# Linear attention and RWKV channel mix: per-engine orders from a list schedule, five units per four batches, and batch 0's time shift mix folded into the attention weights

## The chip, the cores and the metric

The kernel runs on one core of one Trainium2 chip. The metric is device time in microseconds (us) of the whole program; lower is better. Engines are named as in the profile: PE is TensorE (matmuls), PEld its weight loads, DVE is VectorE, ACT is ScalarE, POOL is GpSimd and SP is SyncE, which here only issues transfers. All times inside a run are counted from the start of its profiled span.

## The reference, cut to what matters

```python
# attention, B=8, H=8, S=576, D=64
q_s = softmax(q, axis=-1)                 # over the 64 features
k_s = softmax(k, axis=2)                  # over the sequence
kv  = einsum('bhsd,bhse->bhde', k_s, v)   # k_s^T v, one 64x64 matrix per head
x   = q_s @ kv                            # then heads side by side: (B, S, 512)
# RWKV channel mix, d_model 512, d_ff 1024
x_prev = x shifted down by one row of the sequence, first row 0
xk = mu_k * x + (1 - mu_k) * x_prev
xr = mu_r * x + (1 - mu_r) * x_prev
k  = maximum(xk @ w_k, 0)
v  = (k * k) @ w_v
out = sigmoid(xr @ w_r) * v
```

Inputs and output are float32. In both kernels the large matmuls take bf16. A batch's heads are handled in two groups (group 0 and 1) of four heads.

## The kernel before: the parts that matter

The order of the work is set by hand. A few lines start batch 0; from then on an attention generator advances by small steps between the matmuls of the channel mix, so that TensorE always has channel-mix work while the other engines prepare the next batch.

```python
    UNITS = ((0, 512), (512, 384), (896, 256))      # columns of two batches (2*576)
...
    # the weights are held back until a load of batch 0, group 0 has landed
    def emit_weights(gate):
        ...
                ld = part(wk_bf, moe_w_k, F, u, 512 * h, 512 * h + 512)
                if gate is not None:
                    tc.add_manual_dep(ld.ins, gate.ins.name, SYNC)
...
    # mu comes from one fp32 transpose of an 8x128 tile
    mup = psum.tile([128, 8], F32, tag="mm", bufs=4, name="mup")
    nc.tensor.transpose(out=mup[:], in_=mu_sb[:], identity=identf[:])
...
    # channel mix: every accumulator is a PSUM tile of its own, four in rotation
    def unit(pair, c0, n, step=1):
        for f0 in range(0, FT, step):
            kfps = [psum.tile([128, 512], F32, tag="mm", bufs=4, name="kfp")
                    for _ in range(step)]
            ...                                             # kfp += wk^T xk
                nc.scalar.activation(out=rel[:, 0:n], in_=kfp[:, 0:n], func=ACT.Relu, ...)
                nc.vector.tensor_tensor(out=k2[:, f0 + i, 0:n], in0=rel..., in1=rel..., op=ALU.mult)
        for m in range(n // 128):
            rp = psum.tile([128, C], F32, tag="mm", bufs=4, name="rp")   # xr wr -> tanh
            ...
            vp = psum.tile([128, C], F32, tag="mm", bufs=4, name="vp")   # k2 wv -> times gate -> out
```

The time shift mix of each head group (`diff`, `mix`) is done on VectorE in bf16: difference of neighbouring rows, scale by mu, add.

The softmax here doesn't subtract the row's maximum and nothing guards it: scores larger than these inputs give would overflow.

Of the kernel before, what the change touches and what calls it, by code (L numbers as in the profile page):

```python
# [15 lines left out]


@with_exitstack
def kernel(
# [12 lines left out]






# [9 lines left out]
    UNITS = ((0, 512), (512, 384), (896, 256))  # L47
    assert B % 2 == 0

    const = ctx.enter_context(tc.tile_pool(name="const", bufs=1))  # L50
    ldpool = ctx.enter_context(tc.tile_pool(name="ldpool", bufs=4))
    apool = ctx.enter_context(tc.tile_pool(name="apool", bufs=3))
    xpool = ctx.enter_context(tc.tile_pool(name="xpool", bufs=2))
    mpool = ctx.enter_context(tc.tile_pool(name="mpool", bufs=2))
    opool = ctx.enter_context(tc.tile_pool(name="opool", bufs=3))
    psum = ctx.enter_context(tc.tile_pool(name="psum", bufs=1, space=bass.MemoryType.PSUM))


    raw = {}

    SYNC = mybir.DependencyInfo(mybir.DependencyClass.Sync, mybir.DependencyReason.DATA)
    ctx.enter_context(tc.manual_schedule(engines={mybir.EngineType.Pool}))

    def emit_load(b: int, g: int, queues=None):
        t = ldpool.tile([128, 3, 2, J * D], F32, tag="raw", name="raw")
        ld = []
        for i, src in enumerate((q, k, v)):
            ap = bass.AP(tensor=src.tensor,
                         offset=src.offset + (b * H + 2 * g) * S * D,
                         ap=[[J * D, 128], [4 * S * D, 2], [1, J * D]])  # L70
            queue = queues[i] if queues else nc.gpsimd
            ld.append(queue.dma_start(out=t[:, i, :, :], in_=ap))  # L72
        raw[b, g] = t
        return ld

    first = emit_load(0, 0, (nc.sync, nc.scalar, nc.sync))
    mu_sb = const.tile([8, 128], F32, name="mu_sb")
    for m, src in enumerate((moe_mu_k, moe_mu_r)):
        ap = bass.AP(tensor=src.tensor, offset=src.offset, ap=[[64, 4], [256, 2], [1, 64]])
        nc.sync.dma_start(out=mu_sb[4 * m:4 * m + 4, :].rearrange("p (u e) -> p u e", u=2),  # L80
                          in_=ap)
    emit_load(0, 1, (nc.scalar, nc.sync, nc.scalar))
    warm = const.tile([1, 1], F32, name="warm")
    nc.vector.memset(warm[:], 0.0)
    nc.scalar.activation(out=warm[:], in_=warm[:], func=ACT.Exp)


    ident = const.tile([128, 128], BF16, name="ident")
    make_identity(nc, ident[:])
    identf = const.tile([8, 8], F32, name="identf")  # L90
    nc.vector.tensor_copy(out=identf[:], in_=ident[0:8, 0:8])
    mask = const.tile([128, 128], BF16, name="mask")
    nc.vector.memset(mask[:], 0.0)
    nc.vector.memset(mask[0:64, 0:64], 1.0)
    nc.vector.memset(mask[64:128, 64:128], 1.0)
    vvs, xbs = [], []
    for i in range(3):
        vv = const.tile([128, J, 130], BF16, name=f"vv{i}")
        nc.vector.memset(vv[:, :, 128:130], 1.0)
        vvs.append(vv)  # L100
        xb = const.tile([128, 2, 64 + S], BF16, name=f"xb{i}")
        nc.vector.memset(xb[:, :, 0:1], 0.0)
        xbs.append(xb)

    wk_bf = const.tile([128, CT, F], BF16, name="wk_bf")
    wv_bf = const.tile([128, FT, C], BF16, name="wv_bf")
    wr_bf = const.tile([128, CT, C], BF16, name="wr_bf")

    def emit_weights(gate):
        def part(dst, src, n, u, c0, c1):  # L110
            ap = bass.AP(tensor=src.tensor, offset=src.offset + 4 * u * D * n + c0,
                         ap=[[n, 64], [D * n, CT], [1, c1 - c0]])
            return nc.gpsimd.dma_start(out=dst[64 * u:64 * u + 64, :, c0:c1], in_=ap)

        for h in range(2):
            for u in range(2):
                ld = part(wk_bf, moe_w_k, F, u, 512 * h, 512 * h + 512)
                if gate is not None:
                    tc.add_manual_dep(ld.ins, gate.ins.name, SYNC)
                gate = None  # L120
        for u in range(2):
            part(wr_bf, moe_w_r, C, u, 0, C)
        n = FT // 2
        for h in range(2):
            ap = bass.AP(tensor=moe_w_v.tensor,
                         offset=moe_w_v.offset + h * n * 128 * C,
                         ap=[[C, 128], [128 * C, n], [1, C]])
            nc.gpsimd.dma_start(out=wv_bf[:, h * n:(h + 1) * n, :], in_=ap)

    mu = const.tile([128, 8], F32, name="mu")  # L130

    def emit_mu():
        mup = psum.tile([128, 8], F32, tag="mm", bufs=4, name="mup")
        nc.tensor.transpose(out=mup[:], in_=mu_sb[:], identity=identf[:])  # L134
        nc.vector.tensor_copy(out=mu[:], in_=mup[:])


    xpair = {}
    box = [0]

    class Attention:
        def __init__(self, b: int, g: int):
            self.b, self.g = b, g
            self.t = raw.pop((b, g))
            self.vv = vvs[box[0] % 3]
            self.xb = xbs[box[0] % 3]
            box[0] += 1
            if b // 2 not in xpair:
                xpair[b // 2] = (xpool.tile([128, CT, 2 * S], BF16, tag="xk", name="xk"),
                                 xpool.tile([128, CT, 2 * S], BF16, tag="xr", name="xr"))  # L150
            self.eqk = apool.tile([128, 2, J, 2, D], BF16, tag="eqk", name="eqk")

        def exp(self, i: int):
            nc.scalar.activation(  # L154
                out=self.eqk[:, i, :, :, :],
                in_=self.t[:, i, :, :].rearrange("p u (j d) -> p j u d", d=D),
                func=ACT.Exp)

        def cast_v(self, copy):
            copy(out=self.vv[:, :, 0:128].rearrange("p j (u d) -> p j u d", u=2),  # L160
                 in_=self.t[:, 2, :, :].rearrange("p u (j d) -> p j u d", d=D))

        def norm_q(self):
            eq = self.eqk[:, 0, :, :, :].rearrange("p j u d -> p (j u) d")
            rsum = apool.tile([128, 2 * J], F32, tag="rsum", name="rsum")
            nc.vector.reduce_sum(out=rsum[:], in_=eq, axis=AX.X)  # L166
            rrec = apool.tile([128, 2 * J], F32, tag="rrec", name="rrec")
            nc.vector.reciprocal(out=rrec[:], in_=rsum[:])
            self.qs = apool.tile([128, J, 128], BF16, tag="qs", name="qs")
            nc.vector.tensor_tensor(  # L170
                out=self.qs[:].rearrange("p j (u d) -> p (j u) d", u=2), in0=eq,
                in1=rrec[:, :, None].to_broadcast((128, 2 * J, D)), op=ALU.mult)

        def kv(self, tag: str):
            if tag == "att":
                t = psum.tile([128, 2, 512], F32, tag="att", bufs=2, name="kvp")
                self.kvp = [t[:, 0, :], t[:, 1, :]]
            else:
                self.kvp = [psum.tile([128, 512], F32, tag="mm", bufs=4, name="kvp")[:, :]
                            for _ in range(2)]  # L180
            for j in range(J):
                for hf in range(2):
                    r = slice(64 * hf, 64 * hf + 64)
                    nc.tensor.matmul(  # L184
                        self.kvp[hf][:, 0:129],
                        lhsT=self.eqk[r, 1, j, :, :].rearrange("p u d -> p (u d)"),
                        rhs=self.vv[r, j, 0:129], start=(j == 0), stop=(j == J - 1))

        def weights(self):
            self.w = apool.tile([128, 2, 128], BF16, tag="w", name="w")  # L190
            rz = apool.tile([128, 2], F32, tag="rz", name="rz")
            for hf in range(2):
                nc.vector.reciprocal(out=rz[:, hf:hf + 1], in_=self.kvp[hf][:, 128:129])
            for hf in range(2):
                nc.vector.scalar_tensor_tensor(  # L195
                    out=self.w[:, hf, :], in0=self.kvp[hf][:, 0:128],
                    scalar=rz[:, hf:hf + 1], in1=mask[:], op0=ALU.mult, op1=ALU.mult)

        def transpose_q(self):
            self.qtp = psum.tile([128, 16, 128], BF16, tag="att", bufs=2, name="qtp")  # L200
            for j in range(J):
                nc.tensor.transpose(out=self.qtp[:, j, :], in_=self.qs[:, j, :],  # L202
                                    identity=ident[:])
# [32 lines left out]
    def attention(b: int, g: int):  # L236
# [11 lines left out]
        yield  # L248
        a.x(0)
        yield  # L250
        a.x(1)
        yield
        a.diff()
        a.mix(0)
# [145 lines left out]
```

## Time and profile before

| | before |
|---|---|
| median of 4 runs beside the changed kernel | 221.03 us (220.99 to 221.58) |
| profiled span | 219.7 us |
| first matmul; first kfp; kfp without a break | 9.79; 20.80; 27.82 us |
| unit 1 of the channel mix starts | 49.66 us |
| last matmul ends | 215.1 us |

The page's second section gives the busy tenths of each engine in 40 slices of 5.5 us. These are four of its rows for the kernel before:

```profile
PE   0156599988999999999999999999999999999991
DVE  1196389999999998889798998888787758483431
ACT  2645279999977779676929696949736392644340
DMA  6999999999999791897085220232131400340414
```

TensorE is full from about 30 us to the end, and not before. So the kernel is bound by TensorE, plus a slow start. The timeline of TensorE shows the start (start, duration, engine, line, what, and in brackets the idle time before it and what ended it):

```profile
9.79 0.24 PE L134 MATMUL mup<-identf,mu_sb 8*128 8x8 f32 x1 [9.79 <-DMA mu_sb<-in_moe_mu_r_dram]
10.56 1.16 PE L184 MATMUL kvp<-vv_103,eqk 64*128 64x129 bf16 x18 [0.53 <-ACT vv_103 L160]
...
20.80 2.77 PE L270 MATMUL kfp<-xk,wk_bf 128*128 128x512 bf16 x6
...
27.82 6.73 PE L270 MATMUL kfp<-xk,wk_bf 128*128 128x512 bf16 x23 [2.92 <-DVE xk L232]
...
49.66 1.14 PE L270 MATMUL kfp<-xk,wk_bf 128*128 128x384 bf16 x6
```

The last step before continuous work is VectorE's mix of batch 0, group 1 (`xk`, 2.92 us of waiting). In what follows, the "lost" time of TensorE means this, worked out from the trace's matmul records: from one matmul's start to the next one's start, less the time that its columns take when warm (columns / 2400 us + 0.0025 us; for the 18 kv matmuls and the 9 transposes of a group 0.035 and 0.068 us each, as they follow each other in the busy part of the trace). Before, TensorE loses 7.8 us in the first 20 us, 7.0 from 20 to 40, 2.7 from 40 to 60 and 4.3 in all the rest.

### The profile page before, as it was taken

The numbers are of one execution on the slowest core, as the hardware profiler recorded it, in microseconds if no ns is written. First come the engines' busy times: TensorE is split into PE (matmuls) and PEld (weight loads), VectorE is DVE, ScalarE is ACT, GpSimd is POOL, SyncE is SP. The second block draws the span as 40 slices with busy tenths as digits, with TensorE's granted clock in tenths as the row PEclk, the third lists the DMA queues.
The fourth block names the chain that finished last, engine by engine and source line by source line (L and its number), as shares of the span: only waits on it lengthen the run. The fifth ranks groups of instructions, "written<-read, shape, count | busy, mean of one in ns | idle before, by whom it ended". The sixth has DMA issues, their size and how long they took to land.

```text
span 219.7 us, 3641 instructions
## 1 busy us (share of the span) xinstructions
PE 193.5 (88%) x1313; PEld 101.6 (46%) x1313; DVE 166.3 (76%) x384; ACT 147.7 (67%) x230; POOL 35.8 (16%) x56
## 2 busy tenths in 40 slices
PE   0156599988999999999999999999999999999991
PEld 0134134534547454445557443546465444554650
DVE  1196389999999998889798998888787758483431
ACT  2645279999977779676929696949736392644340
POOL 1294252433431210230030000000000000000000
PEclk9999969999999999999999999999999999999999
DMA  6999999999999791897085220232131400340414
GB/s 215 397 158 199 262 402 388 393 400 403 404 393 406 273 343 71 256 298 288 3 264 201 49 51 0 57 90 48 36 88 24 95 3 22 73 95 5 108 36 95
DMA packets 16171, 40.62 MB, mean 185 GB/s; under 512 B 2072, under 2 KB 4632, under 8 KB 16152
## 3 DMA queue, kind: packets, MB, share of 16 engines
q0 software_dynamic: 8736, 27.40, 38.0%
q1 hardware_dynamic: 6600, 11.22, 18.0%
q10 hardware_dynamic: 816, 1.77, 2.2%
q8 instruction: 10, 0.16, 0.3%
q14 instruction: 9, 0.07, 0.1%
HBM read 33.56 MB, written 9.44 MB: 196 GB/s over the span
## 4 chain that ended last, share of the span: by engine, by line
PE 60%; ACT 19%; DVE 13%; DMA 3%; issue 2%; SPq 1%; DVEq 0%; ACTq 0%
PE vp L291 22%; PE kfp L270 19%; PE rp L284 11%; ACT eqk L154 5%; ACT qt L207 4%; ACT rel L276 4%; DMA mu_sb<-in_moe_mu_r_dram 3%; PE kvp L184 3%; PE qtp L202 3%; PE xp L212 2%; DVE rsum L166 2%; DVE xk L232 2%; DVE qs L170 2%; ACT xb_105 L215 2%; ACT xb_109 L215 1%
## 5 line engine op out<-in xcount | busy, mean ns | idle before, releaser
L270 PE MATMUL kfp<-xk,wk_bf 128*128 128x384 bf16 (+2 forms) x384 | 72.6, 335 | 4.3 <-DVE xk L232 3.7
L276 ACT ACTIVATE rel<-kfp 128x512 bf16<-128x512 f32 (+2 forms) x96 | 45.4, 518 | 20.5 <-PE kfp L270 19.5
L270 PEld LDWEIGHTS <-wk_bf 128*128 128x128 bf16 x384 | 36.3, 99 | 30.3 <-issue 8.5
L154 ACT ACTIVATE eqk<-raw 128x1152 bf16<-128x1152 f32 x32 | 37.5, 1204 | 9.7 <-DMA raw<-in_q_dram 5.9
L294 DVE SCALAR_TENSOR_TENSOR ot<-th,vp 128x512 f32<-128x512 f32 x36 | 24.6, 683 | 17.3 <-PE vp L291 12.5
L287 ACT ACTIVATE th<-rp 128x512 f32<-128x512 f32 x36 | 22.7, 631 | 21.7 <-PE rp L284 20.7
L284 PE MATMUL rp<-wr_bf,xr 128*128 128x512 bf16 x144 | 37.0, 379 | 0.0
L207 ACT COPY qt<-qtp 128x1152 bf16<-128x1152 bf16 x16 | 18.2, 1136 | 7.7 <-PE qtp L202 7.5
L166 DVE TENSOR_REDUCE rsum<-eqk 128x18 f32<-128x1152 bf16 x16 | 21.6, 1348 | 1.6 <-ACT eqk L154 1.5
L170 DVE TENSOR_TENSOR qs<-eqk,rrec 128x1152 bf16<-128x1152 bf16 x16 | 21.7, 1355 | 0.8
L230 DVE TENSOR_SCALAR xm<-xd,mu 128x576 bf16<-128x576 bf16 x64 | 21.6, 378 | 0.4
L284 PEld LDWEIGHTS <-xr 128*128 128x128 bf16 x144 | 13.3, 98 | 13.8
L72 POOL DMA_DIRECT2D raw<-in_q_dram x14 | 10.0, 713 | 52.9 <-ACT vv_111 L160 24.0
L212 PE MATMUL xp<-qt,w 128*128 128x512 bf16 x64 | 13.5, 302 | 2.6 <-ACT qt L207 2.3
L184 PEld LDWEIGHTS <-eqk 64*128 64x128 bf16 x288 | 9.4, 100 | 9.2 <-issue 8.3
L202 PE MATMUL qtp<-ident,qs 128*128 128x128 bf16 x144 | 11.6, 231 | 1.5 <-DVE qs L170 1.5
L202 PEld LDWEIGHTS <-qs 128*128 128x128 bf16 x144 | 9.8, 103 | 4.1 <-DVE qs L170 1.8
L212 PEld LDWEIGHTS <-w 128*128 128x128 bf16 x64 | 6.3, 103 | 11.0 <-issue 6.1
L72 POOL DMA_DIRECT2D raw<-in_v_dram x14 | 10.0, 711 | 8.4 <-DMA raw<-in_q_dram 5.8
L72 POOL DMA_DIRECT2D raw<-in_k_dram x14 | 10.0, 711 | 5.7 <-DMA raw<-in_v_dram 3.0
L195 DVE SCALAR_TENSOR_TENSOR w<-kvp,rz,mask 128x128 bf16<-128x128 f32 x32 | 9.7, 345 | 0.0
L134 PE MATMUL mup<-identf,mu_sb 8*128 8x8 f32 x1 | 0.2, 243 | 9.8 <-DMA mu_sb<-in_moe_mu_r_dram 9.8
(83 smaller groups left out, 238.7 us busy)
## 6 DMA issues: line engine op xcount, KB each, us to landing
out_dram<-ot SPq DMA_DIRECT2D x72, 128.0 KB, 2.4
raw<-in_q_dram POOLq DMA_DIRECT2D x14, 576.0 KB, 12.4
raw<-in_k_dram POOLq DMA_DIRECT2D x14, 576.0 KB, 12.7
raw<-in_v_dram POOLq DMA_DIRECT2D x14, 576.0 KB, 13.1
wk_bf<-in_moe_w_k_dram POOLq DMA_DIRECT2D x4, 256.0 KB, 6.5
wv_bf<-in_moe_w_v_dram POOLq DMA_DIRECT2D x2, 512.0 KB, 12.4
raw<-in_k_dram ACTq DMA_DIRECT2D x1, 576.0 KB, 5.6
raw<-in_q_dram SPq DMA_DIRECT2D x1, 576.0 KB, 5.2
```

Of the source, the lines that this page charges most:

```text
L72: ld.append(queue.dma_start(out=t[:, i, :, :], in_=ap))
L154: nc.scalar.activation(out=self.eqk[:, i, :, :, :], in_=self.t[:, i, :, :].rearrange("p u (j d) -> p j u d", d=D), func=ACT.Exp)
L166: nc.vector.reduce_sum(out=rsum[:], in_=eq, axis=AX.X)
L170: nc.vector.tensor_tensor(out=self.qs[:].rearrange("p j (u d) -> p (j u) d", u=2), in0=eq, in1=rrec[:, :, None].to_broadcast((128, 2 * J, ...
L202: nc.tensor.transpose(out=self.qtp[:, j, :], in_=self.qs[:, j, :], identity=ident[:])
L207: nc.scalar.copy(out=self.qt[:], in_=self.qtp[:, 0:J, :])
L212: nc.tensor.matmul(self.xp[:, 64 * c:64 * e], lhsT=self.w[:, hf, :], rhs=self.qt[:, c:e, 64 * hf:64 * hf + 64], start=True, stop=True)
L270: nc.tensor.matmul(kfp[:, 0:n], lhsT=wk_bf[:, ct, fc * 128:(fc + 1) * 128], rhs=xk[:, ct, c0:c0 + n], start=(ct == 0), stop=(ct == CT - 1))
L276: nc.scalar.activation(out=rel[:, 0:n], in_=kfp[:, 0:n], func=ACT.Relu, scale=HALF_ROOT)
L284: nc.tensor.matmul(rp[:], lhsT=xr[:, ct, c0 + 128 * m:c0 + 128 * m + 128], rhs=wr_bf[:, ct, :], start=(ct == 0), stop=(ct == CT - 1))
L291: nc.tensor.matmul(vp[:], lhsT=k2[:, ft, 128 * m:128 * m + 128], rhs=wv_bf[:, ft, :], start=(ft == 0), stop=(ft == FT - 1))
L294: nc.vector.scalar_tensor_tensor(out=ot[:], in0=th[:], scalar=1.0, in1=vp[:], op0=ALU.add, op1=ALU.mult)
```

## The change

The intent is to shorten the start and to let a program, not a hand, weave the work.

1. Orders. Every operation goes into a `Plan` with an engine, an assumed occupancy and latency, a priority key, its dependences and the buffers that it takes and gives. A greedy list schedule picks, for each engine, the operation that can start earliest, and among equals the smallest key. The kernel then emits the operations in that order.
2. Units of 512 columns: four of 512 and one of 256 per four batches, in place of 512, 384, 256 per two.
3. Batch 0's mix is folded: the kv weights are multiplied by mu and by (1 - mu), and x and x_prev are summed in PSUM by matmuls. That needs mu spread along the free axis on all 128 partitions, which two sets of small float32 selection matmuls produce.
4. Batch 0's and 1's loads are issued in halves, and mu's load goes first on another queue.

The four single accumulators become halves of two-bank tiles, and the wait of the weight loads on batch 0's load is now only in the plan. Core of the diff, with cuts:

```diff
-    UNITS = ((0, 512), (512, 384), (896, 256))
+    UNITS = ((0, 512), (512, 512), (1024, 512), (1536, 512), (2048, 256))
...
+    banks = [psum.tile([128, 2, 512], F32, name=f"bank_{x}") for x in "abcd"]
+    ps = {"mm": [banks[2 + i // 2][:, i % 2, :] for i in range(4)],
+          "att": [t[:, :, :] for t in banks[0:2]], "early": [t[:, :, :] for t in banks[2:4]]}
...
+    pick = const.tile([8, 8, 2, 128], F32, name="pick")
+    flip = const.tile([1, 2, 128], F32, name="flip")
+    ones = const.tile([1, 64], F32, name="ones")
+    mu_slot = [Slot("mm") for _ in range(3)] + [Slot("att")]
+    def emit_mu_rows(m):
+        for s in range(2):                       # s = 0: mu, s = 1: mu - 1
+            for ct in range(CT):
+                for u in range(2):
+                    nc.tensor.matmul(to, lhsT=pick[:, 4 * m + ct, u, :],
+                                     rhs=mu_sb[:, 64 * u:64 * u + 64], start=True, stop=(s == 0), ...)
+                    if s == 1:
+                        nc.tensor.matmul(to, lhsT=flip[:, u, :], rhs=ones[:],
+                                         start=False, stop=True, ...)
+    for m in range(2):
+        o = plan.add("PE", 2.0, 2.2, -450 + 500 * m, lambda m=m: emit_mu_rows(m), [mu_t],
+                     [mu_slot[1 + m]] + mu_slot[3:] * (m == 0))
...
-                if gate is not None:
-                    tc.add_manual_dep(ld.ins, gate.ins.name, SYNC)
+        wk_done.append(plan.add("POOL", 1.25, 1.25, h, lambda h=h: [
+            weight_part(wk_bf, moe_w_k, F, u, 512 * h, 512 * h + 512) for u in range(2)],
+            gate, size=1048.0))                  # gate: in the plan only
...
+            rank = (max(t, now + 0.03), op.key)  # greedy: earliest start, then key
...
+    for op in plan.order():
+        op.emit()
```

## The prediction

> **What bounds it now.** TensorE, behind a slow start. The windows view has TensorE busy 19.4 to 20.0 of every 20 us from 60 us on. In the timeline a warm 512-column matmul starts every 0.216 us; from the trace's matmul records I get 183.6 us of warm TensorE work: 155 of channel mix and about 1.8 for each of 16 head groups. From 30 us to the last matmul at 215.1 only about 8 us are lost; after unit 1 starts (49.66) 5.9. The tail after the last matmul is 4.6 us, and the measured time is 1.35 above the span.
>
> The rest is the start. mu_sb lands only at 9.7 us, behind bulk loads on its queue; group 1's mix is done at 27.8, and only then is TensorE continuous. Early matmuls come 0.43 us apart, twice the warm 0.216: the half-rate state of an idle array (the Trainium skill, "TensorE: Matmul & The Clock Gate", part 1); the trace agrees.
>
> **What changes.** Batch 0's x copy, edge copy, difference, scale and mix (about 4.5 us in a row after x) become four small vector operations on PSUM (0.35 us each, as the w operation now) and one copy per half and mix. mu no longer queues behind v. q of both groups is loaded first, in halves, so the 1.35 us sums and products start earlier. TensorE gains about 3 us of x matmuls and two sets of 24 fp32 matmuls of 64 columns. The Trainium skill ("FP8 and Floating Point Precision", TensorE Precision Notes) gives true fp32 four passes: 0.107 us warm, 0.21 cold, 2.5 to 5 us a set, an estimate. No run shows it yet. The first set falls in idle time, before 11 us.
>
> Estimated start: batch 0's loads still need until about 12.4 us (590 KB in 1.5 us, read from landings). Then v cast 0.8, kv 1.1, weights 1.3 behind other vector work, x 0.8, copy 0.7: group 1's xk at 18 to 19 instead of 27.8. The first w_k half lands at about 16.
>
> **How much is critical.** Not all 9 us. Unit 1 needs batch 1, whose last load lands at about 36 us as now: 12.3 MB at 0.39 MB/us, unchanged by the diff. Unit 0 with batch 1's attention keeps TensorE busy only to about 41. After the last v come cast, kv, weights, x, copies, edge, difference, scale and mix, 6.4 us bare by the trace's durations, on VectorE and ScalarE that are full between 30 and 60 now. I expect unit 1 at about 44 instead of 49.66, with 2 to 4 us of TensorE wait before it. From there 159.6 us of work, 3 of stalls (VectorE still near 87% full, and batch 3 is needed 192 columns earlier than now), tail 4.6, overhead 1.35: **212.5 us**.
>
> Range 208 to 217. Faster by over 2%: 0.83; within 2%: 0.15; slower: 0.02.
>
> **What would show it.** Right: the first long run of kfp matmuls at 17 to 20 us; a TensorE wait before unit 1 between 40 and 46, released by batch 1's mix; VectorE and ScalarE busy unchanged within 5 us. Wrong: the fp32 matmuls hold TensorE beyond 11 us and delay q transposes and kv; batch 1's loads land later than 38; TensorE loses over 5 us after 60, because the fixed orders rest on assumed durations and in-order queues wait for an operation that the plan thought ready.
>
> **What would make it wrong.** Faster than 208: batch 1 ready near 41, no stalls later. Slower than 217: the order mismatches real landings, so that one late vector operation frees no PSUM bank, or the clock falls to half again in the wait before unit 1.

## The result, and the profile after

| | before | after |
|---|---|---|
| median | 221.03 us | 251.13 us (250.79 to 251.24, 4 runs) |
| ratio | | 1.1345, 95% interval 1.132 to 1.137 |
| profiled span | 219.7 | 249.3 |
| first kfp; unit 1 | 20.80; 49.66 | 38.72; 71.67 |
| last matmul ends | 215.1 | 244.4 |

A ratio here is the mean time of one kernel's fast runs over the mean of the other's fast runs of the same rounds, so it is not quite the ratio of the medians that stand beside it.

The change made the kernel 13.4% slower. The same rows of the page, with the granted clock of TensorE:

```profile
PE   0899889999478999989989998899999999999992
DVE  4920153588997998898999999998944233252331
ACT  4410255699968988998689885566235144244150
PEclk9999999999959999999999999999999999999999
DMA  6999999059999679976510132120240330431413
```

TensorE is busy almost from the start (8 and 9 tenths from the second slice, that is from 6 us; a slice is 6.2 us here), where before it had 1, 5, 6, 5. But VectorE and ScalarE are nearly idle from 12 to 31 us (2, 0, 1 and 1, 0, 2), and the transfer engines stop for one slice (the 0 at about 44 to 50 us). The 5 in the clock row stands for a stretch at half rate around the start of unit 1 (the clock records in the trace say 68.9 to 75.7 us); it comes back below. The kernel before has such a stretch from 27.7 to 31.1 us, in unit 0, and none at unit 1. So TensorE is busy early with something that nobody downstream can use. Its timeline names it:

```profile
7.29 0.24 PE L294 MATMUL bank_c<-identf,mu_sb 8*128 8x8 f32 x1 [7.29 <-DMA mu_sb<-in_moe_mu_r_dram]
7.39 3.65 PE L305 MATMUL bank_c<-mu_sb,pick 8*128 8x64 f32 x16
...
17.80 1.14 PE L419 MATMUL bank_b<-ident,qs_a 128*128 128x128 bf16 x9
18.87 3.67 PE L305 MATMUL bank_d<-mu_sb,pick 8*128 8x64 f32 x16
...
28.74 0.63 PE L309 MATMUL bank_a<-ones,flip 1*128 1x64 f32 x2
29.30 1.16 PE L405 MATMUL bank_c<-vv_a,ek_a 64*128 64x129 bf16 x18
...
38.72 1.03 PE L593 MATMUL bank_c<-xk,wk_bf 128*128 128x512 bf16 x4
...
44.13 1.02 PE L593 MATMUL bank_c<-xk,wk_bf 128*128 128x512 bf16 x4 [0.31 <-ACT rel_b L578]
```

The two sets of float32 selection matmuls run from 7.39 to 17.8 and from 18.87 to 29.3 us; only the nine transposes of one q group stand between them. Batch 0's kv, which came at 10.56 us before, starts at 29.30. The groups by form give the cost (busy us, then mean ns of one recorded instruction):

```profile
L305 PE MATMUL bank_a<-mu_sb,pick 8*128 8x64 f32 x32 | 10.1, 416 | 0.0
L309 PE MATMUL bank_a<-ones,flip 1*128 1x64 f32 x32 | 10.1, 416 | 0.0
```

There are 16 such matmuls of each kind into bank_a in the program, and 32 records: one float32 matmul of 64 columns is two instructions. They start 0.2135 us apart, so one matmul costs 0.427 us of TensorE, a set of 24 takes 10.3 us, both 20.5. The bf16 matmuls around them are at half rate too, as shown further below; no run has these float32 matmuls at full rate. ScalarE shows the second-order damage:

```profile
29.40 0.60 ACT L316 ACTIVATE mu_mask<-bank_a 128x512 f32<-128x512 f32 x1 [15.31 <-PE bank_a L309]
...
42.99 0.60 ACT L578 ACTIVATE rel_a<-bank_c 128x512 bf16<-128x512 f32 x1 [0.66 <-PE bank_c L593]
43.48 0.59 ACT L578 ACTIVATE rel_b<-bank_c 128x512 bf16<-128x512 f32 x1
...
48.95 0.70 ACT L375 ACTIVATE eq_c<-raw_g 128x576 bf16<-128x576 f32 x1
```

The first (1 - mu) mask was complete in PSUM at 17.8 us, but ScalarE reads it only at 29.40, because the second set writes the other half of the same two-bank tile, and everything behind it in ScalarE's order waits too. (This is read from the trace and the code; no run changed it alone while the sets were float32.) Batch 1's first exp (`eq_c`) then stands behind batch 0's relu and starts at 48.95. GpSimd issues the next load into that buffer only afterwards, at 51.56 us after 15.69 us without an issue, which is the hole in the transfers.

There is a second, quieter difference in the last line of TensorE's excerpt. The kfp matmul at 44.13 writes bank_c's half 0. Its previous reader, `rel_a`, ended at 43.59. The matmul waits for `rel_b`, which reads the other half and ends at 44.07.

Finally, the weights are no longer held back. This is GpSimd's timeline, first of the kernel before and then of the changed one:

```profile
9.64 2.62 POOL L113 DMA_DIRECT2D wk_bf<-in_moe_w_k_dram  x4 [8.33 <-DMA raw<-in_v_dram]
```

```profile
3.25 2.51 POOL L333 DMA_DIRECT2D wk_bf<-in_moe_w_k_dram  x4
```

They are issued 6.4 us earlier and share the transfers with batch 0; v of batch 0, group 1 landed at 17.3 us, before at 12.7.

### The profile page after: what moved, and what is told of

It is laid out like the page before. It is cut to its first block, busy times and chain, and to the rows that moved or that the text cites. A ratio compares the mean times of both kernels' runs of the same rounds, so it can differ in the third digit from the quotient of the medians.

```text
span 249.3 us, 3772 instructions
## 1 busy us (share of the span) xinstructions
PE 220.9 (89%) x1377; PEld 120.0 (48%) x1377; DVE 164.7 (66%) x371; ACT 150.1 (60%) x228; POOL 39.2 (16%) x64
## 4 chain that ended last, share of the span: by engine, by line
PE 63%; DVE 16%; ACT 12%; issue 4%; DMA 2%; POOL 0%; DVEq 0%; ACTq 0%; POOLq 0%
PE bank_c L593 11%; PE bank_c L634 10%; PE bank_d L634 9%; PE bank_d L593 9%; PE bank_d L624 6%; PE bank_c L624 4%; PE bank_a L309 3%; PE bank_a L305 3%; DVE qs_a L397 2%; DMA mu_sb<-in_moe_mu_r_dram 2%; PE bank_b L419 2%; ACT rel_b L578 2%; DVE ot_c L640 2%; PE bank_d L305 1%; PE bank_c L305 1%
## 5 line engine op out<-in xcount | busy, mean ns | idle before, releaser
L593 PE MATMUL bank_c<-xk,wk_bf 128*128 128x512 bf16 (+1 forms) x176 | 39.2, 357 | 0.7 <-ACT rel_b L578 0.3
L593 PE MATMUL bank_d<-xk,wk_bf 128*128 128x512 bf16 (+1 forms) x144 | 34.7, 372 | 3.0 <-DVE ot_a L640 0.7
L624 PE MATMUL bank_d<-wr_bf,xr 128*128 128x512 bf16 x84 | 21.5, 378 | 0.9 <-ACT rel_c L578 0.6
L634 PEld LDWEIGHTS <-k_a 128*128 128x128 bf16 x144 | 13.5, 98 | 16.8 <-issue 1.8
L634 PEld LDWEIGHTS <-k_b 128*128 128x128 bf16 x144 | 13.6, 97 | 16.0 <-issue 1.2
L634 PE MATMUL bank_d<-wv_bf,k_a 128*128 128x512 bf16 x72 | 18.3, 379 | 0.9 <-ACT th_b L629 0.6
L634 PE MATMUL bank_d<-wv_bf,k_b 128*128 128x512 bf16 x72 | 18.5, 379 | 0.7 <-ACT th_a L629 0.6
L634 PE MATMUL bank_c<-wv_bf,k_b 128*128 128x512 bf16 x72 | 18.0, 379 | 0.2
L634 PE MATMUL bank_c<-wv_bf,k_a 128*128 128x512 bf16 x72 | 18.0, 379 | 0.0
L624 PE MATMUL bank_c<-wr_bf,xr 128*128 128x512 bf16 x60 | 15.4, 379 | 0.3 <-ACT rel_c L578 0.3
```

Source lines behind the costliest of these rows:

```text
L593: nc.tensor.matmul(bank(kf)[:, 0:n], lhsT=wk_bf[:, ct, fc * 128:(fc + 1) * 128], rhs=xs[0][:, ct, c0:c0 + n], start=(ct == 0), stop=(ct == ...
L624: nc.tensor.matmul(bank(rps), lhsT=xs[1][:, ct, c:c + 128], rhs=wr_bf[:, ct, :], start=(ct == 0), stop=(ct == CT - 1))
L634: nc.tensor.matmul(bank(vps), lhsT=k2s[k2.index][:, ft, 128 * m:128 * m + 128], rhs=wv_bf[:, ft, :], start=(ft == 0), stop=(ft == FT - 1))
```

## The experiments

So four suspects: the float32 sets, the shared PSUM tiles, the missing gate of the weights, and the greedy order itself, which rests on assumed durations and no longer matches the machine. The rivals to the first were that TensorE was free enough for it and that the fold or the new units cost the time. Sixteen kernels were run; all gave correct results. A table of all stands at the end of this section.

### e1_bf16: selection matmuls in bf16

```diff
-    pick = const.tile([8, 8, 2, 128], F32, name="pick")     # flip and ones likewise
+    pick = const.tile([8, 8, 2, 128], BF16, name="pick")
+    mu_b = const.tile([8, 128], BF16, name="mu_b")
...
+        nc.vector.tensor_copy(out=mu_b[:], in_=mu_sb[:])
-                                     rhs=mu_sb[:, 64 * u:64 * u + 64], start=True,
+                                     rhs=mu_b[:, 64 * u:64 * u + 64], start=True,
```

> The only difference is the type of the selection matmuls that spread mu (pick, flip, ones and a copy of mu in bf16 in place of fp32); every engine keeps the order of the changed kernel. Theory A (the fp32 selection matmuls hold TensorE from 7.4 to 29.3 us, and the rest of the loss follows from that late start): each matmul falls from 0.427 us to 0.05 to 0.11, both sets together from 20.5 us to 3 to 5, unit 0's kfp start at 17 to 21 us instead of 38.7, and the time falls from 251 to 211 to 219 us. Theory B (the orders of the list schedule and the ungated weight loads are a loss of their own): the start is earlier but TensorE still loses 15 us or more after 40 us; time 225 to 240.

Measured: 235.71 us, ratio to the kernel before 1.0639 (1.0616 to 1.0661). TensorE's timeline:

```profile
7.57 0.58 PE L307 MATMUL bank_c<-mu_b,pick 8*128 8x64 bf16 x8
7.96 0.24 PE L307 MATMUL bank_a<-mu_b,pick 8*128 8x64 bf16 x1
```

One record per matmul, 0.053 us apart: a set lasts from 7.57 to about 8.8 us, 1.2 us. The orders are the same, so the difference of 15.4 us is the price of float32 and what follows from it. The first kfp comes at 23.7 us, unit 1 at 57.1 in place of 71.7. The rest, 14.7 us over the kernel before, has other causes.

### e2_gate and e3_bf16_gate: the weights wait for batch 0 again

```diff
+        ld = nc.gpsimd.dma_start(out=dst[64 * u:64 * u + 64, :, c0:c1], in_=ap)
+        if not gated:
+            tc.add_manual_dep(ld.ins, issued[0, 0, 2, 1].ins.name, SYNC)
+            gated.append(ld)
```

> The changed kernel with one added wait: the first weight load waits for batch 0 group 0's v, as in the kernel before; the change only gates it in its plan, and the trace shows the weights issued at 3.25 us and v of group 1 landing at 17.3 us instead of 12.7. Theory A: TensorE is held until 29.3 us anyway, so the time moves by less than 1.5 us from 251. Rival (bandwidth taken from batch 0 by early weights is a main cause): 3 us or more faster.

> Both edits together. With TensorE free, v of group 1 (17.3 us ungated, about 12.5 gated) should be what group 1's kv waits for. If so this is 2 to 4 us below the bf16 run alone, about 209 to 216 us. If batch 1's loads or VectorE set the start of unit 1, as my prediction had it, the gate is worth under 1 us.

Measured: the gate alone 250.73 us (1.1322), nothing to speak of, because v lands before the float32 matmuls are done either way. The gate on top of bf16: 234.48 us (1.0591, 1.0572 to 1.0611), 1.2 us better than e1; the first kfp comes at 21.0 in place of 23.7 us. So the gate is worth about 1 us, and only once TensorE is free to use it.

### e4_nofold: batch 0's mix on VectorE, as before

```diff
-ON_PE = (0,)
+ON_PE = ()
-    mu_masked = []                # and both sets of selection matmuls, masks and their constants
-    ...
```

> Fold off: batch 0 goes the way of the other batches (x copy, difference, scale, mix) and no selection matmul or mask is made; list schedule, five units and halved loads stay, weights ungated. Theory A: 214 to 222 us, near the kernel before, since only the fold's fp32 matmuls cost. Theory B: 228 or more, because the schedule's orders lose time by themselves.

Measured: 238.3 us (1.0761, 1.0734 to 1.0788). Without fold and without any selection matmul the kernel is still 17 us slower than before. Neither the fold nor float32 explains this part.

### e5_split and e6_bf16_gate_split: four accumulators of one bank each

```diff
-    banks = [psum.tile([128, 2, 512], F32, name=f"bank_{x}") for x in "abcd"]
-    ps = {"mm": [banks[2 + i // 2][:, i % 2, :] for i in range(4)], ...
+    banks = [psum.tile([128, 2, 512], F32, name=f"bank_{x}") for x in "ab"]
+    singles = [psum.tile([128, 512], F32, name=f"mm_{x}") for x in "abcd"]
+    ps = {"mm": [t[:, :] for t in singles], "att": [t[:, :, :] for t in banks]}
```

> The changed kernel with one edit: the four PSUM accumulators are four tiles of one bank each instead of the halves of two two-bank tiles; same orders, fp32 selection matmuls kept. Theory C (a wait is tracked for the whole tile, so a matmul into one half waits for the ScalarE or VectorE read of the other half; this makes four buffers act as two and costs TensorE about 10 of the 16 us by which units slip behind the plan between 25 and 170 us): 238 to 244 us instead of 251. Rival D (the plan's durations are too short and the in-order queues are simply tight, VectorE and ScalarE near full): 249 to 251.

> Separate accumulators together with the bf16 selection matmuls and the gate. Theory A with C: 219 to 226 us, from 234.5 with shared tiles. D: 233 to 235.

Measured: e5 238.65 us (1.0767, 1.0738 to 1.0795), 12.5 us less than the changed kernel with float32 kept. e6, all three repairs, 222.16 us (1.0024, 0.9981 to 1.0067): level with the kernel before. From e3 to e6 the split is worth 12.3 us, so it adds to the float32 cost and does not overlap with it. The timelines of e5, TensorE and ScalarE:

```profile
41.43 0.59 PE L603 MATMUL mm_a<-xk,wk_bf 128*128 128x512 bf16 x2
41.86 0.59 PE L603 MATMUL mm_b<-xk,wk_bf 128*128 128x512 bf16 x2
42.29 0.59 PE L603 MATMUL mm_c<-xk,wk_bf 128*128 128x512 bf16 x2
42.72 0.59 PE L603 MATMUL mm_d<-xk,wk_bf 128*128 128x512 bf16 x2
43.15 0.59 PE L603 MATMUL mm_a<-xk,wk_bf 128*128 128x512 bf16 x2
```

```profile
42.06 0.60 ACT L588 ACTIVATE rel_a<-mm_a 128x512 bf16<-128x512 f32 x1 [0.22 <-PE mm_a L603]
```

A pair of matmuls now starts every 0.43 us without a break, and the relu of mm_a starts while TensorE is already writing mm_b; in the changed kernel the first relu of this stage waited until the whole two-bank tile was written (42.99, after kfp into both halves). The Trainium skill ("PSUM — Partial Sum Buffer", section "PSUM bank collisions raise a hardware error") says that accesses of two engines to different banks run clean and that what has to be guarded is one bank in one group of 32 partitions. The two halves are different banks (512 float32 columns fill a bank of 2 KiB, the same page), so the wait guarded nothing that the hardware needs: e5 leaves it out and its results are correct.

### e7_before_pairs and e8_before_singles: only the tiles, in the kernel before

If shared tiles cost time, they must do so in the hand-ordered kernel as well. e7 makes its four rotating accumulators halves of two tiles; e8, the control, gives it four fixed single tiles in the same way.

```diff
+    mm_pairs = [psum.tile([128, 2, 512], F32, name=f"mm_{x}") for x in "ab"]
+    mm_of = [mm_pairs[i // 2][:, i % 2, :] for i in range(4)]     # e8: four tiles [128, 512]
-            kfps = [psum.tile([128, 512], F32, tag="mm", bufs=4, name="kfp") for _ in range(step)]
+            kfps = [mm() for _ in range(step)]                    # rp, vp, kvp, mup likewise
```

> The kernel before, with its four accumulators handed out in turn from the halves of two two-bank tiles. Theory C: slower than 221.4 by 6 to 15 us, although nothing else is changed. D: within 1 us of 221.4.

> Control for the last: the same turn-taking from four separate one-bank tiles. Both theories: within 1 us of the kernel before; if it is slower, the turn-taking and not the sharing is what the paired run measures.

Measured: e7 250.05 us (1.1293, 1.1248 to 1.1338), e8 221.44 us (0.9996, 0.9974 to 1.0018). e7 and e8 differ only in the two lines that make the tiles, so the shape of the tiles alone costs 28.6 us. From e7's list of TensorE's waits (what waited, for what; us in total, times, longest):

```profile
PE mm_b L275 <- ACT rel L281: 4.5, 9, 1.1
PE mm_a L275 <- ACT rel L281: 3.6, 7, 0.8
PE mm_a L296 <- ACT rel L281: 1.2, 2, 0.8
PE mm_b L296 <- ACT rel L281: 0.6, 2, 0.4
```

None of the four is in the list of the kernel before, whose longest waits for an accumulator add up to less than 1 us. L296 is the vp matmul; with a tile of its own it had no wait for a relu in the list. These lines hold only the longer waits; by the matmul records TensorE in e7 loses 0.5 to 2.9 us in almost every 10 us to the end, where before it loses nearly nothing.

### e9_hold: batch 2 behind batch 1

With the three repairs TensorE still loses 9.5 us between 40 and 60 us, and unit 1 starts at 53.7. VectorE's timeline in e6:

```profile
42.28 1.34 DVE L403 TENSOR_REDUCE rsum_a<-eq_b 128x18 f32<-128x1152 bf16 x1
...
46.81 1.35 DVE L411 TENSOR_TENSOR qs_a<-eq_b,rrec_a 128x1152 bf16<-128x1152 bf16 x1
...
48.28 1.33 DVE L403 TENSOR_REDUCE rsum_b<-eq_c 128x18 f32<-128x1152 bf16 x1
...
52.79 0.75 DVE L555 TENSOR_TENSOR xk<-xm_c,xb_b 128x1152 bf16<-128x1152 bf16 x1
```

The first three are the softmax sums and products of batch 2, 1.34 us each. The last is the mix of batch 1, group 1, for which unit 1 waits. The greedy rule takes whatever can start first, so the next batch's long operations slip in ahead of the short chain that matters. e9 adds a dependence to the plan (and only there): batch 2's exps and casts after batch 1's x copies, batch 2's sums after batch 1's last xk mix.

```diff
+        hold_act = evs_of[1, 1] if b == 2 else []
+        hold_dve = mixed[1, 1, 0] if b == 2 else []
...
-                         [expq[-1]], [stat] if one else [])
+                         [expq[-1]] + hold_dve, [stat] if one else [])     # exps and casts: + hold_act
```

> e6_bf16_gate_split with one addition to the plan: batch 2's exp, cast and sums may not be placed before batch 1 group 1's x copies (ScalarE) and mix (VectorE). In e6 unit 1 starts at 53.7 us, 4 us later than in the kernel before, and TensorE idles from 43.7, because ScalarE and VectorE run batch 2's operations ahead of batch 1's. Theory E (that gap is the reason why the repaired kernel is no faster): unit 1 at 47 to 50 us and 217 to 219 us in all, from 222.2. Rival F (VectorE and ScalarE have too little room for batches 1 to 7 at any order, so the gap only moves to a later unit): unit 1 earlier by 2 to 6 us, but the time within 1 us of 222.2.

Measured: 220.57 us (0.9964, 0.9943 to 0.9984). Unit 1 starts at 45.2, 8.5 us earlier than in e6, but only 1.6 us arrive at the end: the last matmul comes 168.4 us after the start of unit 1, in e6 162.4. Part of this is the marker and not the machine. In e9 only the first two matmuls of unit 1, which need group 0 alone, start at 45.2; the next come at 49.2, after a wait of 3.4 us for group 1's mix, whereas in e6 unit 1 goes on without such a wait. The mix itself ends at 49.2 in place of 53.5, 4.4 us earlier. At the first kfp of unit 2 (75.5 us, in e6 78.6) 3.1 us are left of it. That the held work of batch 2 takes the rest is argued and not shown.

### e10_mask_hold and e15_mask_only: a mask tile for each set, true durations, and the hold for every batch

e15 takes e6, gives the second set's (1 - mu) its own two-bank tile, lets the plan place the second set right behind the first, and tells it what e1 measured for a set. e10 adds the hold, on VectorE alone and for every batch from 2 on.

```diff
-    mu_slot = [Slot("mm") for _ in range(3)] + [Slot("att")]
+    mu_slot = [Slot("mm") for _ in range(3)] + [Slot("att"), Slot("att")]
-        o = plan.add("PE", 2.0, 2.2, -450 + 500 * m, ...
+        o = plan.add("PE", 0.64, 0.84, -450 + 10 * m, ...      # plan doubles it while cold
# e10 only
+        hold_dve = mixed[b - 1, 1, 0] if b >= 2 else []
```

> e6 with the sums of every batch held until the batch before is mixed, the two sets' fourth PSUM use in separate tiles (in e6 ScalarE waits 1.2 us for the second set's matmuls before it can read the first set's mask from the other half of the tile) and true durations for the selection matmuls in the plan. E: 215 to 218 us. F: 220 to 222.5.

> e10 without the hold (the mask's own tile and the true durations of the selection matmuls stay). If the hold made e10's gain: 220.5 to 222.5, unit 1 at 52 to 54 us. If the mask tile did: 216 to 218.

Measured: e15 222.27 us (1.0041, 1.0016 to 1.0066), the same as e6. e10 216.71 us (0.9804, 0.9781 to 0.9828). It is the best kernel, 2.0% faster than the kernel before with an interval of 1.7 to 2.2% (so it is faster, but whether by 2% is unclear), and faster than the changed kernel by 34 us. The mask tile and durations alone earned nothing; adding the hold to them made the gain of 5.6 us. Part of it is clock: by the clock records TensorE is at half rate for 13.6 us in e15, 10.2 in e6 and 3.4 in e10 at this place, and by the matmul records the half rate costs 3.1 us of TensorE between 40 and 60 us in e15 and 1.1 in e10. VectorE in e10:

```profile
47.54 0.75 DVE L558 TENSOR_TENSOR xk<-xm_c,xb_b 128x1152 bf16<-128x1152 bf16 x1
...
48.65 1.33 DVE L404 TENSOR_REDUCE rsum_a<-eq_b 128x18 f32<-128x1152 bf16 x1
```

Batch 1's mix is done first and 5.2 us earlier than in e6. Not all is gained, as TensorE's timeline of e10 shows:

```profile
45.72 0.61 PE L616 MATMUL mm_b<-xk,wk_bf 128*128 128x512 bf16 x2
48.34 0.59 PE L616 MATMUL mm_b<-xk,wk_bf 128*128 128x512 bf16 x2 [2.02 <-DVE xk L558]
49.96 1.16 PE L420 MATMUL bank_a<-vv_b,ek_b 64*128 64x129 bf16 x18 [1.03 <-ACT vv_b L397]
51.05 1.89 PE L616 MATMUL mm_a<-xk,wk_bf 128*128 128x512 bf16 x4
```

At 48.3 to 50.0 TensorE's order has batch 2's kv ahead of unit 1's next kfp, and kv waits for a cast of v. After that the four kfp at 51.05 take 1.89 us; four warm ones take 1.03 (after, at 38.72). So the clock has fallen to half rate as well (49.7 to 53.1 us by the clock records), here after the two waits. TensorE loses 7.8 us between 40 and 60 and about 1 us after that.

### e11_nofold_split, e14_nofold_hold and e12_six_units: what the fold and the units are worth

e11 is e4 with the gate and single tiles, to be set beside e6; e14 is the same with e10's hold, to be set beside e10. e12 is e6 with the unit widths of the kernel before.

```diff
# e11, e14
-ON_PE = (0,)
+ON_PE = ()
# e12
-    UNITS = ((0, 512), (512, 512), (1024, 512), (1536, 512), (2048, 256))
+    UNITS = ((0, 512), (512, 384), (896, 256), (1152, 512), (1664, 384), (2048, 256))
```

> e6 without the fold: batch 0 mixed on VectorE as the others, no selection matmuls; gate and separate accumulators kept. What the fold itself is worth: in shared tiles it was 2.6 us (238.3 without, 235.7 with bf16 selection). If the start counts, 225 to 230; if batch 1 sets unit 1 whatever unit 0 does, within 1.5 us of 222.2.

> e10's hold without the fold. The fold saves if this is slower than e10 (216.7): I expect 216 to 219, since without the hold the kernel without the fold was 1.5 us faster than with it, and unit 1's start depends on batch 1. A time below 216 says that the fold costs.

> e6 with the units of the kernel before (512, 384 and 256 columns for each two batches) in place of five for four batches. Unit 1 needs 128 columns less and batch 3 is needed later. If the unit sizes cost: 218 to 221 us. If they do not: within 1 us of 222.2, the extra unit's relus and squares adding a little.

Measured: e11 220.69 us (0.9969, 0.9952 to 0.9986), so without the hold the fold costs 1.5 us. e14 218.07 us (0.9854, 0.9824 to 0.9883), so with the hold it earns 1.4 us. Both differences are at the edge of the noise (in each pair the intervals overlap slightly), and e11 and e14 make batch 0's kv weights in four vector operations, where the other batches take one. Either way it is a small term: what stands before unit 1 is batch 1, not batch 0. e12 222.11 us (1.0047, 1.0017 to 1.0077), as e6: these intervals show no cost and no gain of the number of units.

### e13_hold_both: ScalarE held as well

```diff
-        hold_act = [] if b >= 2 else []
+        hold_act = evs_of[b - 1, 1] if b >= 2 else []
```

> e10 with ScalarE's exps and casts of a batch held too, until the batch before has its x copies. In e10 TensorE still loses 7.8 us between 40 and 60 us: kv of batch 2 stands ahead of unit 1's kfp and waits for casts whose loads land at 48.8. If that order is the rest of the gap: 212 to 215.5 us, unit 1's second kfp without the 2.0 and 1.0 us waits. If ScalarE is then late for batch 2 instead: 216 to 219.

Measured: 217.58 us (0.9829, 0.9799 to 0.986), no better than e10. Unit 1 starts at 43.9, the earliest of all, and the last matmul ends 166.7 us after it, in e10 165.0. Moving the hold moves the loss. Which order would remove it is not found here.

### e16_best_fp32: the best kernel with float32 selection

```diff
-    pick = const.tile([8, 8, 2, 128], BF16, name="pick")     # flip, ones, mu_b likewise
+    pick = const.tile([8, 8, 2, 128], F32, name="pick")
```

> e10 with the selection matmuls in fp32 again, same orders. Both sets stand before kv in TensorE's order; each took 10.3 us, 20.5 in all against 2.5. Expected 232 to 236 us: 15 to 19 us more than e10, as the start moves and nothing makes it good later.

Measured: 231.67 us (1.0464, 1.0435 to 1.0493), so float32 costs 15.0 us in the otherwise repaired kernel. The first kfp starts at 36.9.

### All runs in one table

Unit 1 is the start of its first kfp; the last column is from there to the end of the last matmul. Both are of the profiled run, the time is the median. The kernel before had medians from 221.03 to 221.46 us.

| run | us | ratio | unit 1 | unit 1 to last matmul |
|---|---|---|---|---|
| before | 221.03 | 1 | 49.7 | 165.5 |
| after | 251.13 | 1.1345 | 71.7 | 172.7 |
| e1 bf16 | 235.71 | 1.0639 | 57.1 | 172.0 |
| e2 gate | 250.73 | 1.1322 | 71.4 | 173.1 |
| e3 bf16, gate | 234.48 | 1.0591 | 54.4 | 173.2 |
| e4 no fold | 238.3 | 1.0761 | 58.7 | 172.6 |
| e5 split | 238.65 | 1.0767 | 69.4 | 162.5 |
| e6 bf16, gate, split | 222.16 | 1.0024 | 53.7 | 162.4 |
| e9 e6 + hold of batch 2 | 220.57 | 0.9964 | 45.2 | 168.4 |
| e10 e15 + hold on VectorE | 216.71 | 0.9804 | 45.7 | 165.0 |
| e11 no fold, gate, split | 220.69 | 0.9969 | 52.7 | 160.9 |
| e12 e6 with six units | 222.11 | 1.0047 | 53.2 | 161.8 |
| e13 e10 + hold on ScalarE | 217.58 | 0.9829 | 43.9 | 166.7 |
| e14 e10 without fold | 218.07 | 0.9854 | 49.9 | 162.7 |
| e15 e6 + mask tile, durations | 222.27 | 1.0041 | 53.7 | 162.8 |
| e16 e10 with float32 | 231.67 | 1.0464 | 61.7 | 163.6 |

(e7 and e8 are the kernel before with other tiles, 250.05 and 221.44 us.) The two columns separate the causes. Float32 moves unit 1 by 15 to 17 us and changes the rest by 1.4 us at most. The split takes 10 to 11 us from the rest and 1 to 2 from the start. The hold moves the marker by 8 us and gives 2 to 6 of them back later; part of that is the marker's, because in e9, e10, e13 and e16 unit 1's first two matmuls run ahead of the mix of batch 1, group 1 (in e10 the third waits until 48.3).

## Why the prediction was wrong, point by point

The prediction's sum was: unit 1 at 44, then 159.6 us of work, 3 of stalls, a tail of 4.6 and 1.35 of overhead, 212.5 us. In the profiled run of the changed kernel the same terms were: unit 1 at 71.7; from there to the last matmul 172.7, which is 13.1 us over 159.6; a tail of 4.9; overhead 1.9; in sum 251.2. So two terms failed, unit 1 by 27.7 us and the stalls by about 10, and the tail and the overhead held within 0.6. The term of 159.6 us was the kernel before's; by the matmul records the changed kernel has 157.2 us of work after unit 1 and loses 15.5, so the stalls were missed by 12.5 and the work hid 2.4 of it.

**Unit 1 at 44: the float32 term.** The step that failed is "2.5 to 5 us a set, an estimate" and "the first set falls in idle time, before 11 us". A set takes 10.3 us. The estimate took four passes from the Trainium skill ("FP8 and Floating Point Precision", TensorE Precision Notes): four times 64 columns at the early rate of 0.43 us per 512 columns makes 0.213 us, and that is exactly the distance of two recorded instructions. But each matmul is two such instructions, 0.427 us. Eight times the bf16 time (0.053 us in e1), not four, is what these traces show for this form. The upper end of the estimate was thus half of the truth. It also assumed idle time for the first set only and did not ask where the second set stands: ahead of batch 0's kv in TensorE's order, so it falls on the critical path too: in e1 the sets are 18 us shorter, and 15.4 us of that arrive at the end. The prediction named this very case as what would show it wrong ("the fp32 matmuls hold TensorE beyond 11 us"), and it happened. e1, e5 to e6 and e16 put the term at 15.0 to 16.5 us; e5 to e6 contains the gate's 1 us.

A second cost sat in the same place. The prediction named the half rate of an idle array for the early matmuls but did not ask when it ends. The Trainium skill ("TensorE: Matmul & The Clock Gate", part 1) says that about 3.4 us of sustained activity lift it. Here 22 us of nearly unbroken float32 matmuls did not lift it: the 18 kv matmuls that followed at 29.30 took 1.16 us, warm they take 0.70, and the x matmuls ran at half rate up to about 38 us. The clock row of the page shows 9 there, but only because it counts time without a clock record as full: the first record of this trace begins at 38.2 us, with full rate, just where the spacing of the matmuls becomes warm. Before it the rate has to be read from the spacing. That the small operands (8 or 1 rows) do not count as activity would explain it, but no run here varied the rows with the float32 type kept, so it stays a supposition.

**Unit 1 at 44: the order.** With float32, gate and tiles repaired, unit 1 came at 53.7 and not at 44. The prediction counted batch 1's chain bare, 6.4 us after its last load, "on VectorE and ScalarE that are full", and took for granted that batch 1 goes first there. The greedy rule lets batch 2's sums go first; holding them brought the start of unit 1 to 45.7 (e10). The marker flatters this: all of batch 1 is mixed only at 48.3. The step that failed is the way from batch 1's last load to unit 1, 8 us in the prediction (36 to 44, 6.4 of it bare). The load landed at 36.0 us in the changed kernel, as predicted, but from the last load to the end of the mix it takes 17.2 us in e6 and still 10.9 in e10. The rule was in the diff to be read: the rank is the earliest start and only then the key. That start was gated by batch 1 and not by batch 0 was right, and so was that little of the fold's saving would reach the end: it is worth 1.4 us with the hold, minus 1.5 without. The first long kfp, predicted at 17 to 20 us, comes at 21.6 in e6 and 20.4 in e13. The prediction that VectorE and ScalarE stay within 5 us of their busy time held too: 166.3 and 147.7 us before, 164.7 and 150.1 after.

**The 3 us of stalls.** The prediction never looked at the allocation of PSUM. It says nothing of the diff's line that makes accumulators halves of `bank_c` and `bank_d`. That line costs 12.4 us here and 28.6 us in the kernel before (e7). With single tiles the time from unit 1 on is 162.4 us in e6, next to the predicted 159.6 plus 3. That agreement is partly luck: by the matmul records it is 157.0 us of work and 5.4 lost, since part of batch 2's attention already lies before unit 1. Of the 5.4 us, 2.0 are half rate: the prediction's own warning that "the clock falls to half again in the wait before unit 1" came true in the changed kernel (68.9 to 75.7 us) and in e6 (47.5 to 57.7, with unit 1 starting at 53.7):

```profile
53.70 1.90 PE L612 MATMUL mm_d<-xk,wk_bf 128*128 128x512 bf16 x4
```

Four such matmuls take 1.03 us warm. The prediction's warning about late operations that free no bank named the symptom, not the cause.

**The loads.** The prediction took for granted that batch 0's loads land as before. The gate on the weights was in the diff as a `gate` argument that only the plan uses. That cost 0.4 us alone and 1.2 us when TensorE is free, so it mattered little.

**The plan believed in the same errors.** Running the kernel's own scheduler, which is part of the kernel and knows no chip, gives a plan that ends at 211.2 us, close to my 212.5, and its first relu at 22.16; on the chip that relu came at 42.99. Plan and prediction agreed because both took 2 to 2.5 us warm for a set and neither knew of the shared tiles.

**What stays open.** e10 is 4.2 us above the prediction. By its profiled run (217.73 us, 1.0 above the median) unit 1 is 1.7 us later than predicted, from there to the last matmul it takes 165.0 us, 2.4 us over 159.6 plus 3, and tail and overhead are 1.1 longer; the loss lies between 40 and 60 us, where batch 2's kv waits ahead of unit 1's kfp. e13 shifted it and did not remove it. Why e13 is 3 us faster than e9, which differs in the mask tile, the durations and the hold of later batches, was not taken apart; the half-rate stretch at unit 1 is shorter in e13 (48.5 to 51.9 us) than in e9 (48.1 to 54.9), which by the matmul records is 0.9 us of it. e15 shows only that mask tile and durations earn nothing without the hold.

## What to carry to other kernels

When a diff regroups PSUM accumulators into larger tiles, count what waits for what by tile and not by bank, in both directions: a matmul into one half waited here for ScalarE's reading of the other. A tiny float32 matmul can cost as much as a large bf16 one (64 columns took 0.427 us here, as 512 bf16 columns did at the same rate); price them by a measured record, and ask not only whether TensorE is idle but what stands behind them in its order. A schedule that a program makes is only as good as its durations and its tie rule, so compare its planned start of a few marker operations with the trace, and see whether the next batch's work overtakes the last operation that the present one waits for. A marker such as "first matmul of unit 1" can move without the work moving, so check what follows it.

## What the Trainium skill lacked or had wrong

- "FP8 and Floating Point Precision", TensorE Precision Notes: it gives four passes for true float32 but neither the number of instructions nor a time. Here a matmul of 64 float32 columns was two recorded instructions 0.2135 us apart, 0.427 us in all, and the same matmul in bf16 at the same early rate 0.053 us: a factor of eight, not four.
- "TensorE: Matmul & The Clock Gate", part 1: it says that some 3.4 us of sustained activity lift the half rate. 22 us of float32 matmuls with 8 or 1 rows, nine transposes between them, did not (kv 1.16 us after them, 0.70 us warm; the first clock record, with full rate, begins at 38.2 us). The page does not say whether such small matmuls count.
- No page says that waits are kept per PSUM tile and not per bank by the layer this kernel is written in. "PSUM — Partial Sum Buffer" gives only what the hardware needs, one bank in one group of 32 partitions; guarding two banks as one tile cost 28.6 us of 221 in e7, and 12.3 to 12.5 us in the changed kernel.
